# An attention and gated-MLP block on one core: the streamed gate and up weights are issued on GpSimd's queue, with other assumed landing times and another scheduling table

## The chip, the cores and the metric

The kernel runs on one NeuronCore of a Trainium2 chip. Its time is the device time of one execution in microseconds (us). A profile of one execution gives, for every engine, what ran when: PE is TensorE (matrix multiply), ACT is ScalarE (activation functions), DVE is VectorE (elementwise), POOL is GpSimd, SP is SyncE, which here issues nearly all DMAs.

## The reference

The block has 2048 tokens of width 512, 32 heads of 16, and a hidden width of 1792.

```python
mod = (silu(c) @ w_mod)            # six vectors of 512: sa, ca, ga, sb, cb, gb
h = layernorm(x) * (1 + ca) + sa
q, k, v = heads(h @ wqkv)          # 32 heads of 16
x = x + ga * (softmax(q k^T / 4) v) @ wo
h = layernorm(x) * (1 + cb) + sb
x = x + gb * ((gelu(h @ w_gate) * (h @ w_up)) @ w_down)
```

## The kernel before

**Scores and Exp.** For a set of 128 to 512 queries (`SETS`) and a group of four heads, PE makes scores, transposed, in tiles of 128 keys by 512 columns in PSUM (`ps_sc`, six banks). There are 2048 such tiles. Most go to ACT, which takes the Exp of two or three tiles in one instruction into `E` (`128x1024` or `128x1536`, line 377). The others go to DVE in groups of four ("quads"): DVE turns the four score tiles into 16-bit patterns that stand for powers of two (line 389, `128x512` from `ps_sc`, into `kq` buffers, which partly lie in the regions `dreg`, `mreg` and `onorm`), and three instructions of `128x2048` add a constant to those patterns (`sq` buffers). Each tile is then multiplied by the values on PE (`ps_pv`, from `E,vaug`, or from a DVE buffer and `vs`).

**Softmax sums.** A unit of four heads ends with a copy to `osb` and a chain: DMA of the sums to `den`, a reciprocal on DVE, a store to DRAM (`scr_rec`), four loads that spread it (`rb`), a product on DVE (`onorm`), and later four DMAs that merge head halves (`onorm<-onorm`). In semaphore names these are `db`, `dc`, `dd`, `de`.

**The MLP beside it.** When all of a query set's heads are done, its output projection, layer norm and MLP run on PE, ACT and DVE between the scores of later sets. For the first six sets (`FLOW`) gate and up weights are streamed: `load` in `side_ffn` fetches 256 columns (256 KB) into one of two buffers for each of the two matrices (`wst`, in `mreg`; semaphores `st...`), a new one each time PE has used a buffer up. Each of these sets fetches seven gate and seven up pieces. Later sets find their weights loaded.

**The order.** The program is written out in full by a planner. `stream` goes through the score tiles and keeps a model of when each engine is free and when each DMA has landed. It decides which tiles go to ACT and which to DVE, when a piece of MLP work is put between scores, and when a filler matmul (`xs,ident` or `xs,zero`, whose result is overwritten or nought) keeps PE going. `MARGIN` and `EARLY` add nanoseconds to the assumed landing time of a kind of DMA. `TUNE` holds one row of fourteen limits for each stage of 64 tiles. Engines carry out their rows strictly in order, and a row that waits for a semaphore holds up what stands behind it on its engine.

Of the kernel before, what the change touches and what calls it, by code (L numbers as in the profile page):

```python
# [13 lines left out]
P = 128  # L14
# [36 lines left out]
FLOW = sum(a + n <= 1536 for a, n in SETS)  # L51
ISSUE = {"dd": 462, "de": 630, "db": 610, "dc": 400, "st": 410, "sd": 530, "se": 530, "ws": 450, "wu": 420, "wg": 510, "wd": 480, "ou": 400, "qo": 620}
SAFE = 0
EARLY = (1500, 2500, 2000)
MARGIN = {"db": 1200, "dd": 1800, "de": 1500, "qo": 1500, "st": 1500, "sd": 1700, "se": 1700, "wd": 1700, "wu": 1500, "wg": 1500}
FIRST = (2, 1, 2, 3)
STOP = ('ln2',)
STOPAT = 0
# [2 lines left out]
STEP = 64  # L61
RULES = (600, 3500, 6, 120, 700, 150, 2, 9, 96, 30, 2, 1536, 100, 150)
TUNE = (
# [33 lines left out]
)  # L97
END = (0, None)
WAIT = 250
# [29 lines left out]
class _Recorder:  # L129
# [292 lines left out]
    def dma(self, eng, out, in_, sem, noncontig=False, late=0):  # L422
# [8 lines left out]
        run = min(int(a.ap[-1][1]) * mybir.dt.size(a.dtype) for a in (out, in_))  # L431
        return self.rec(eng, fn, [in_], [out], dma=sem, cost=(n, run, MARGIN.get(sem[:2], 0) + late))

# [36 lines left out]
class _Kernel(_Recorder):  # L470
# [696 lines left out]
    def side_ffn(self, gi, part=None):  # L1167
# [15 lines left out]
        def load(x, i):  # L1183
            if not flow or (i >= NFC // 2 and gi == FLOW - 1) or self.dry:
                return
            v = (self.B_w_gate, self.B_w_up)[x].rearrange("(a p) n -> p a n", p=P)
            b, k, i = (first + i) % 2, gi + i // (NFC // 2), i % (NFC // 2)
            self.task([("sp", lambda: self.dma("sp", self.wst[x][b], v[:, :, 2 * P * i:2 * P * i + 2 * P], "st%d%d" % (x, b)))],
                      ("wl", k, x, i))

        def load_down(i):
# [5 lines left out]
        if gi == 0:  # L1197
            yield from self.until(("wdg", 6))
            for i in range(2):
                load(0, i)  # L1200
                load(1, i)
# [4 lines left out]
        def up(x, ci, sub):  # L1206
            for s, fc in enumerate(sub):
                yield from self.until(("wl", gi, x, fc // 2) if flow else ("wr", x, fc // 2))
                for dci in range(NDC):
                    if flow:  # L1210
                        lhs = self.wst[x][(first + fc // 2) % 2][:, dci, P * (fc % 2):P * (fc % 2) + P]
                    else:
                        lhs = self.up_w((self.wg, self.wu)[x], fc, dci)
                    yield W, lambda s=s, lhs=lhs, dci=dci: self.mm(
                        mi[:, W * s:W * s + W], lhs, self.t2T[:, dci, c0:c0 + W], start=(dci == 0), stop=(dci == NDC - 1), whole=W == P)
                if fc % 2:
                    load(x, fc // 2 + 2)
# [220 lines left out]
    def rules(self, i):  # L1438
        self.tune = TUNE[min(i, len(TUNE) - 1)]

# [385 lines left out]
    def unit_end(self, u, acc):  # L1826
# [17 lines left out]
        sem = b + 4 * (o > 0)  # L1844
        late = EARLY if qd < 6 else (0, 0, 0)
        s2 = self.scr2[b, P * o:P * o + 4 * L]
# [261 lines left out]
```

## Time and profile before

| | |
|---|---|
| three executions | 808.4, 812.86, 815.13 us; median 812.86 |
| profiled execution | 810.3 us, of which 808.6 lie between its first and last instruction (the span) |
| granted TensorE clock | 0.996 |
| busy | PE 750.5 us (93%), DVE 752.3 (93%), ACT 776.8 (96%), POOL 4.6 (1%) |
| DMA | 60.92 MB, 75 GB/s on average |

The three shares are near each other. What sets the end is read from the chain of work that ended last and from the idle time of ACT in each stretch of the run.

### The profile page before, as it was taken

The numbers are of one execution on the slowest core, as the hardware profiler recorded it, in microseconds if no ns is written. First come the engines' busy times: TensorE is split into PE (matmuls) and PEld (weight loads), VectorE is DVE, ScalarE is ACT, GpSimd is POOL, SyncE is SP. The second block draws the span as 40 slices with busy tenths as digits, with TensorE's granted clock in tenths as the row PEclk, the third lists the DMA queues.
The fourth block names the chain that finished last, engine by engine and source line by source line (L and its number), as shares of the span: only waits on it lengthen the run. The fifth ranks groups of instructions, "written<-read, shape, count | busy, mean of one in ns | idle before, by whom it ended". The sixth has DMA issues, their size and how long they took to land.

```text
span 808.6 us, 37540 instructions
## 1 busy us (share of the span) xinstructions
PE 750.5 (93%) x17260; PEld 374.8 (46%) x17264; DVE 752.3 (93%) x1521; ACT 776.8 (96%) x734; POOL 4.6 (1%) x13
## 2 busy tenths in 40 slices
PE   8899999998989998999999999988999999989998
PEld 4333334433544454444543554344434554446666
DVE  7877899999999999999999999999998999999973
ACT  6999999999999999999999999999999999999972
POOL 2000000000000000000000000000000000000000
PEclk9999999999999999999999999999999999999999
DMA  9100112221541144104420442043223622200000
GB/s 295 66 15 8 25 50 74 75 58 32 148 145 29 39 128 134 34 16 133 129 65 16 140 121 54 22 128 114 62 64 104 189 83 76 71 10 13 18 12 15
DMA packets 97904, 60.92 MB, mean 75 GB/s; under 512 B 16913, under 2 KB 95378, under 8 KB 97746
## 3 DMA queue, kind: packets, MB, share of 16 engines
q1 hardware_dynamic: 97216, 57.99, 25.2%
q8 instruction: 135, 2.21, 1.1%
q10 hardware_dynamic: 530, 0.53, 0.2%
q14 instruction: 23, 0.19, 0.1%
HBM read 51.74 MB, written 4.18 MB: 69 GB/s over the span
## 4 chain that ended last, share of the span: by engine, by line
ACT 81%; PE 13%; DVE 3%; DMA 2%; issue 1%; SPq 0%; DVEq 0%
ACT E L377 78%; PE ps_sc L364 5%; PE ps_mi L364 4%; PE ps_pv L364 3%; ACT wreg L377 3%; DMA scr_rec<-rden 1%; DMA xs<-in_A_x_dram 0%; DVE mreg L389 0%; DMA mreg<-in_B_w_up_dram 0%; SPq L427 0%; DMA rb<-scr_rec 0%; DVE st L417 0%; DVE wreg L398 0%; DVE hreg L389 0%; PE ps_mi L368 0%
## 5 line engine op out<-in xcount | busy, mean ns | idle before, releaser
L377 ACT ACTIVATE E<-ps_sc 128x1024 bf16<-128x1024 f32 (+2 forms) x688 | 750.8, 1295 | 17.8 <-PE ps_sc L364 17.2
L364 PE MATMUL ps_sc<-qo,kT 32*128 32x256 bf16 (+2 forms) x2048 | 202.0, 273 | 19.8 <-ACT E L377 17.6
L364 PE MATMUL ps_sc<-qT,kT 32*128 32x256 bf16 (+3 forms) x2048 | 202.0, 274 | 17.7 <-ACT E L377 14.3
L364 PE MATMUL ps_pv<-E,vaug 128*17 128x256 bf16 (+2 forms) x3168 | 151.5, 274 | 2.7 <-DVE vaug L398 1.1
L389 DVE TENSOR_SCALAR dreg<-ps_sc 128x512 uint16<-128x512 f32 x204 | 138.2, 687 | 4.6 <-PE ps_sc L364 4.0
L364 PE MATMUL ps_mi<-wreg,mreg 128*32 128x256 bf16 x2816 | 110.0, 275 | 5.2 <-DVE wreg L398 1.7
L364 PEld LDWEIGHTS ps_sc<-qT,kT 32*128 32x128 bf16 (+1 forms) x2048 | 62.7, 92 | 109.8 <-ACT E L377 89.4
L364 PEld LDWEIGHTS ps_sc<-qo,kT 32*128 32x128 bf16 x2048 | 63.1, 92 | 106.5 <-ACT E L377 87.7
L364 PEld LDWEIGHTS ps_pv<-E,vaug 128*17 128x17 bf16 x3168 | 61.0, 89 | 58.9 <-issue 40.8
L389 DVE TENSOR_SCALAR kq<-ps_sc 128x512 uint16<-128x512 f32 x112 | 76.3, 688 | 8.0 <-PE ps_sc L364 7.4
L364 PEld LDWEIGHTS ps_mi<-wreg,mreg 128*32 128x32 bf16 x2816 | 64.1, 96 | 38.6 <-issue 21.5
L364 PE MATMUL ps_pv<-mreg,vs 128*17 128x256 bf16 (+2 forms) x1544 | 69.6, 267 | 0.5 <-issue 0.5
L389 DVE TENSOR_SCALAR mreg<-ps_sc 128x512 uint16<-128x512 f32 x100 | 67.7, 687 | 1.7 <-PE ps_sc L364 1.2
L389 DVE TENSOR_SCALAR mreg<-dreg 128x2048 uint16<-128x2048 uint16 x91 | 61.5, 686 | 0.0
L364 PEld LDWEIGHTS ps_pv<-mreg,vs 128*17 128x17 bf16 x1544 | 35.2, 91 | 9.6 <-issue 3.4
L364 PE MATMUL ps_mi<-hreg,wreg 128*32 128x512 bf16 (+1 forms) x496 | 37.3, 382 | 0.4 <-DVE vaug L398 0.2
L381 DVE TENSOR_TENSOR wreg<-wreg 128x1024 bf16<-128x1024 bf16 (+1 forms) x56 | 34.6, 618 | 0.0
L394 DVE SCALAR_TENSOR_TENSOR wreg<-wreg,ps_mi 128x512 bf16<-128x512 bf16 x49 | 33.5, 683 | 0.6 <-PE ps_mi L364 0.2
L398 DVE CAST wreg<-ps_mi 128x512 bf16<-128x512 f32 x49 | 33.6, 686 | 0.5 <-PE ps_mi L364 0.2
L389 DVE TENSOR_SCALAR mreg<-mreg 128x2048 uint16<-128x2048 uint16 x46 | 31.1, 684 | 0.0
L389 DVE TENSOR_SCALAR mreg<-kq 128x2048 uint16<-128x2048 uint16 x45 | 30.7, 686 | 0.1
L377 ACT ACTIVATE wreg<-wreg 128x1024 bf16<-128x1024 bf16 (+1 forms) x28 | 29.8, 1065 | 0.0
(202 smaller groups left out, 786.9 us busy)
## 6 DMA issues: line engine op xcount, KB each, us to landing
mreg<-in_B_w_up_dram SPq DMA_DIRECT2D x46, 256.0 KB, 3.1
mreg<-in_B_w_gate_dram SPq DMA_DIRECT2D x42, 256.0 KB, 3.7
dreg<-wd_scaled SPq DMA_DIRECT2D x18, 256.0 KB, 3.4
rb<-scr_rec SPq DMA_DIRECT2D x116, 32.0 KB, 2.0
mreg<-wd_scaled SPq DMA_DIRECT2D x12, 256.0 KB, 4.2
ereg<-wd_scaled SPq DMA_DIRECT2D x12, 256.0 KB, 4.1
mreg<-in_w_mod_dram SPq DMA_DIRECT2D x1, 2048.0 KB, 12.2
out_dram<-xs SPq DMA_DIRECT2D x15, 128.0 KB, 2.0
```

Source lines behind the costliest of these rows:

```text
L364: return self.rec("pe", lambda e: e.matmul(out, lhsT, rhs, start=start, stop=stop, tile_position=tp), [lhsT, rhs], [out], cost=(n, int(rhs ...
L377: return self.rec("act", lambda e: e.activation(out, in_, func, scale=scale, **kw), rd, wr, cost=self.cost("act", out, [in_], "act"))
L381: return self.rec(eng, lambda e: e.tensor_tensor(out, a, b, op), [a, b], [out], cost=self.cost(eng, out, [a, b], "tt"))
L389: return self.rec(eng, lambda e: e.tensor_scalar(out, a, s1, s2, **kw), rd, [out], cost=self.cost(eng, out, [a], "ts") + 60 * (len(rd) - 1 ...
L394: return self.rec("dve", lambda e: e.scalar_tensor_tensor(out, a, s, b, op0=op0, op1=op1), rd, [out], cost=self.cost("dve", out, [a, b], " ...
L398: return self.rec(eng, lambda e: e.tensor_copy(out, in_), [in_], [out], cost=self.cost(eng, out, [in_], "ts"))
```

## The change

Three things are edited. The DMA of a streamed gate or up piece is issued by GpSimd ("pool") instead of SyncE. The assumed landing times change: `EARLY`, which adds to the sums' DMAs of most units, falls; the store of the reciprocals (`dc`), the store of the scaled down weights (`ws`), the streamed pieces (`st`) and the streamed down weights (`sd`) get more. And the rows of `TUNE` are others (33 rows before and after; one line of each is shown).

```diff
-EARLY = (1500, 2500, 2000)
-MARGIN = {"db": 1200, "dd": 1800, "de": 1500, "qo": 1500, "st": 1500, "sd": 1700, "se": 1700, "wd": 1700, "wu": 1500, "wg": 1500}
+EARLY = (800, 1000, 800)
+MARGIN = {"db": 1200, "dd": 1800, "de": 1500, "qo": 1500, "st": 2300, "dc": 1500, "ws": 1500, "sd": 2000, "se": 1700, "wd": 1700, "wu": 1500, "wg": 1500}
...
 TUNE = (
+    (1000, 4097, 6, 120, 700, 150, 2, 9, 96, 30, 2, 1536, 100, 150),
...
-    (450, 4097, 6, 300, 1100, -100, 1, 9, 96, 30, 4, 1536, 100, 150),
...
-            self.task([("sp", lambda: self.dma("sp", self.wst[x][b], v[:, :, 2 * P * i:2 * P * i + 2 * P], "st%d%d" % (x, b)))],
+            self.task([("sp", lambda: self.dma("pool", self.wst[x][b], v[:, :, 2 * P * i:2 * P * i + 2 * P], "st%d%d" % (x, b)))],
```

Since the planner writes the whole program, nearly every stretch comes out in another order. Three places show what matters.

On SP, at the first query set's MLP, this is the difference between the two programs (`in_B_w_gate` and `in_B_w_up` are the streamed pieces, `wd_scaled` the down weights, `den` belongs to the chain of the sums, and `qo`, `qT` are copies that split the next queries into head halves):

```order
-L427 DMA mreg<-in_B_w_gate_dram 128x4x256
 L427 DMA dreg<-wd_scaled 128x2x512 x2
-L427 DMA mreg<-in_B_w_gate_dram 128x4x256
 L427 DMA onorm<-onorm 16x3x256 x4
-L427 DMA mreg<-in_B_w_gate_dram 128x4x256
 L427 DMA qo<-qT 16x4x256 x4
-L427 DMA mreg<-in_B_w_gate_dram 128x4x256
 L427 DMA dreg<-wd_scaled 128x2x512
 L427 DMA mreg<-wd_scaled 128x2x512
 L427 DMA den<-osb 128x1x16
 L427 DMA qT<-qo 16x4x256 x4
-L427 DMA mreg<-in_B_w_up_dram 128x4x256 x2
```

The streamed pieces no longer stand between the other DMAs of SP. On POOL, whose last work before was a small mask, the changed program goes on like this:

```order
L408 AFFINE_SELECT self<-self 128x128
L427 DMA mreg<-in_B_w_gate_dram 128x4x256
L427 DMA mreg<-in_B_w_up_dram 128x4x256
L427 DMA mreg<-in_B_w_gate_dram 128x4x256
L427 DMA mreg<-in_B_w_up_dram 128x4x256
L427 DMA mreg<-in_B_w_gate_dram 128x4x256 x4
L427 DMA mreg<-in_B_w_up_dram 128x4x256 x2
```

In all, 84 pieces (42 of gate, 42 of up) move from SP to POOL.

On ACT, these are the last Exp instructions ahead of the table load that precedes the end of the program, before:

```order
L377 ACTIVATE E<-ps_sc 128x1024 x4
L377 ACTIVATE E<-ps_sc 128x1536 x2
L377 ACTIVATE E<-ps_sc 128x1024 x4
L377 ACTIVATE E<-ps_sc 128x1536 x6
L377 ACT_TABLE_LOAD
```

and of the change:

```order
L377 ACTIVATE E<-ps_sc 128x1024 x7
L377 ACTIVATE E<-ps_sc 128x1536
L377 ACTIVATE E<-ps_sc 128x1024 x4
L377 ACTIVATE E<-ps_sc 128x1536 x8
L377 ACTIVATE E<-ps_sc 128x512
L377 ACT_TABLE_LOAD
```

More score tiles reach ACT here, and one Exp of a single tile is new. Over the whole program ACT has 389 Exp of 1024 columns (412 before), 287 of 1536 (268 before) and one of 512 that was not there; DVE has 408 conversions of a score tile (420 before) and 306 of its `128x2048` additions (315 before).

On PE, this stands between the last scores and the end of the last softmax products, before:

```order
L364 MATMUL ps_sc<-qo,kT 128x128 x12
L364 MATMUL ps_pv<-mreg,vs 17x128 x16
L368 MATMUL ps_mi<-ident,hreg 128x128 x2
L364 MATMUL ps_sc<-xs,ident 32x512 x4
L364 MATMUL ps_pv<-E,vaug 17x128 x32
L364 MATMUL ps_pv<-dreg,vaug 17x128 x16
L364 MATMUL ps_pv<-ereg,vs 17x128 x16
L364 MATMUL ps_pv<-mreg,vs 17x128 x16
L364 MATMUL ps_pv<-E,vaug 17x128 x16
L364 MATMUL ps_pv<-mreg,vs 17x128 x16
```

and of the change:

```order
L364 MATMUL ps_sc<-qo,kT 128x128 x4
L364 MATMUL ps_pv<-E,vaug 17x128 x16
L364 MATMUL ps_pv<-mreg,vs 17x128 x16
L368 MATMUL ps_mi<-ident,hreg 128x128 x2
L364 MATMUL ps_sc<-self,osb 128x4
L364 MATMUL ps_sc<-xs,ident 32x512 x4
L364 MATMUL ps_sc<-wo,onorm 32x512 x4
L364 MATMUL ps_pv<-E,vaug 17x128 x16
L364 MATMUL ps_pv<-ereg,vs 17x128 x16
```

Behind the last scores stand 64 products into `ps_pv` instead of 128.

58 rows, old and new, of the table TUNE are left out of this document.

## The prediction

> **What bounds the kernel now.** I read the profile's first part and its chain first, then each engine's busy time in ten stretches, then the rows that carry prices.
>
> ```profile
> PE 750.5 (93%) x17260; PEld 374.8 (46%) x17264; DVE 752.3 (93%) x1521; ACT 776.8 (96%) x734; POOL 4.6 (1%) x13
> ACT 81%; PE 13%; DVE 3%; DMA 2%; issue 1%; SPq 0%; DVEq 0%
> ```
>
> Three engines are nearly full, but the chain that ended last lies on ACT for 81% of the span. SP's queue has none of it to speak of. The stretches (columns: length, then busy us of PE, PEld, DVE, ACT, POOL) show where ACT is not busy:
>
> ```profile
> 0.00:13.26 13.26, 11.34 (x90) 5.57 (x95) 8.84 (x35) 6.15 (x14) 4.33 (x12) 1.00 0.91 259
> 13.26:100.00 86.74, 79.39 (x1412) 30.19 (x1407) 71.60 (x187) 85.64 (x79) 0.31 (x1) 0.98 0.17 53
> 100.00:200.00 100.00, 93.65 (x2149) 40.44 (x2145) 97.41 (x190) 100.00 (x93) 0.00 (x0) 1.00 0.22 61
> 200.00:300.00 100.00, 93.15 (x2242) 47.89 (x2246) 96.72 (x183) 98.80 (x94) 0.00 (x0) 1.00 0.34 97
> 300.00:400.00 100.00, 93.04 (x2213) 46.49 (x2201) 96.98 (x182) 99.81 (x94) 0.00 (x0) 1.00 0.32 91
> 400.00:500.00 100.00, 93.93 (x2180) 46.34 (x2180) 98.15 (x184) 100.00 (x96) 0.00 (x0) 1.00 0.29 79
> 500.00:600.00 100.00, 93.15 (x2160) 44.99 (x2156) 98.93 (x187) 100.00 (x96) 0.00 (x0) 1.00 0.28 76
> 600.00:700.00 100.00, 94.16 (x2130) 46.99 (x2126) 96.50 (x186) 98.68 (x92) 0.00 (x0) 0.98 0.35 101
> 700.00:781.25 81.25, 75.48 (x2382) 46.18 (x2375) 75.24 (x160) 80.58 (x73) 0.00 (x0) 1.00 0.10 26
> 781.25:808.60 27.35, 23.23 (x361) 19.76 (x351) 11.91 (x34) 7.10 (x13) 0.00 (x0) 1.00 0.04 12
> ```
>
> 13.26 is the start of the first Exp, 781.25 the table load behind the last one. Between them ACT is idle for 1.10 + 1.20 + 0.19 + 1.32 + 0.67 = 4.5 us out of 768. The head (13.3 us) and the end (27.4 us) are other chains. So **the span is head + ACT's work + 4.5 us + end**: a change gains at most 4.5 us by taking waits away, and anything above that must come out of ACT's work or the end.
>
> **The work that moves.** The new order has 412 - 23 Exp of 1024 columns, 268 + 19 of 1536 and one more of 512; that is 12 score tiles more on ACT and 12 fewer on DVE.
>
> ```profile
> L377 ACT ACTIVATE E<-ps_sc 128x1024 bf16<-128x1024 f32 x412 | 413.8, 1137 | 2.3 <-PE ps_sc L364 2.2
> L377 ACT ACTIVATE E<-ps_sc 128x1536 bf16<-128x1536 f32 x268 | 394.8, 1560 | 2.8 <-PE ps_sc L364 2.3
> L377 ACT ACTIVATE E<-ps_sc 128x512 bf16<-128x512 f32 x6 | 3.5, 598 | 9.4 <-PE ps_sc L364 9.4
> L377 ACT ACTIVATE E<-ps_sc 128x1024 bf16<-128x1024 f32 (+2 forms) x688 | 750.8, 1295 | 17.8 <-PE ps_sc L364 17.2
> ```
>
> Neighbours on ACT overlap: the two large forms' means add up to 412 x 1.137 + 268 x 1.560 = 886.5 us, while the group as a whole (last row, less 4 us for the small ones) is busy for 746.8. The overlap is 139.7 / 680 = 0.205 us each, so an instruction really costs 0.932 and 1.355 us, and a 512 one 0.598 - 0.205 = 0.393. The sum: -23 x 0.932 + 19 x 1.355 + 0.393 = **+4.7 us on ACT**. This is the bottleneck's own work and nothing hides it.
>
> ```profile
> L389 DVE TENSOR_SCALAR dreg<-ps_sc 128x512 uint16<-128x512 f32 x204 | 138.2, 687 | 4.6 <-PE ps_sc L364 4.0
> L389 DVE TENSOR_SCALAR mreg<-dreg 128x2048 uint16<-128x2048 uint16 x91 | 61.5, 686 | 0.0
> L364 PE MATMUL ps_sc<-xs,ident 128*32 128x512 bf16 x52 | 4.8, 386 | 1.6 <-ACT E L377 1.6
> ```
>
> DVE loses 12 conversions at 0.687 us and 9 additions at 0.686: **-14.4 us on DVE**, which gains nothing as long as ACT is fed. PE gets 48 more pieces of filler (36 in `ps_sc`, 12 in `ps_mi`), at 4.8 / 52 = 0.09 us each 4.4 us, in 58 us of PE's idle time. The planner puts fillers into score banks only where ACT's work reaches further than PE's, so more of them speak for a plan in which PE waits for ACT, not the reverse. At the end, 64 products into `ps_pv` fewer stand behind the last scores:
>
> ```profile
> 780.72 0.89 PE ps_pv L364 x63
> ```
>
> That row of the chain gives 0.89 / 63 = 0.014 us each: **-0.9 us**. The rest of the end has nearly the same rows.
>
> **The loads that move to POOL.** 84 issues leave SP.
>
> ```profile
> L427 SPq DMA_DIRECT2D mreg<-in_B_w_up_dram x46: 367/432/1385, 178.8 to 666.4; - x46
> DMA to landing us min/median/max: 2.8/3.1/5.5
> SPq L427 <- PE ps_mi L364: 62.3, 31, 7.2
> PE ps_mi L364 <- DMA mreg<-in_B_w_up_dram: 1.6, 1, 1.6
> PEld ps_mi L364 <- DMA mreg<-in_B_w_gate_dram: 0.6, 1, 0.6
> PE ps_mi L364 <- DMA mreg<-in_B_w_gate_dram: 0.3, 1, 0.3
> ```
>
> SP is spared about 84 x 0.432 = 36 us of issuing (duration: minimum, median, maximum ns) and most of 62.3 us in which such a load waited for PE to leave its buffer, with the sums' DMAs queued behind it. That is worth only what somebody waited for: PE waited for these weights three times, 2.5 us in all, though landings took up to 5.5 us. Behind a load on POOL stand only other such loads, and only PE waits for them. How long POOL takes to issue one, and how long it then takes to land, no row shows. Nearest are SP's 0.432 us and, for POOL's own work, 0.31 and 2.27 us:
>
> ```profile
> 55.77 0.31 POOL L408 TENSOR_SCALAR_AFFINE_SELECT self<-self 128x128 f32<-128x128 f32 x1 [50.48 <-DVE self L405]
> 2.17 2.27 POOL L405 MEMSET vaug<- 128x512 bf16 x1
> ```
>
> From below: the three waits go, at most 2.5 us gained. From above: each landing later by 2.27 - 0.43 = 1.8 us, which can cost PE 84 x 1.8 = 155 us if no load had slack. I take 0: two buffers per matrix give slack, as three waits in 84 loads show, and this price is nearest to SP's row, the same transfer. Both ends count for the range.
>
> **The other assumed landings.** `EARLY` and `MARGIN` move no data by themselves; they move rows. What was added over the sums' chain was 1200 + 1500 + 0 + 1800 + 2500 = 7.0 us, and is now 2.0 + 1.5 + 2.8 = 6.3.
>
> ```profile
> 221.47 4.71 DMA scr_rec<-rden
> 227.03 1.31 SPq L427
> 228.38 2.07 DMA rb<-scr_rec
> DVE onorm L381 <- DMA rb<-scr_rec: 1.2, 1, 1.2
> ```
>
> The first three rows, of the chain in order of time, show one late store and a busy SP queue behind it; DVE waited 1.2 us for it, the only such wait. If the plan now comes too early, DVE stands at `onorm`, with conversions queued behind it and ACT's score banks behind these: at worst 1.2 us for each of the 29 products, 35 us; at best the 1.2 us goes. I take 0, nearest to the one wait seen.
>
> **The sum.** 808.6 + 4.7 - 0.9 = 812.4 us of span, with today's 4.5 us of ACT's waits unchanged. The execution lasts 1.7 us longer than its span (810.3): 814.1 us. The profiled execution is 2.6 us below the median shown (812.86), so I put the forecast at 815.
>
> **A rule against the change.** A `128x2048` addition takes DVE 0.686 us, as long as 512 columns out of PSUM: a fourfold rate. The Trainium skill ("SBUF — State Buffer", Who interferes with whom) says that VectorE at such a rate and GpSimd lock one another out of a shared port pair for a whole instruction, and that descriptors which GpSimd writes for its own DMAs are starved by it. No run here has POOL and DVE so mixed; by it, loads land later or DVE stands, as the first rival has it.
>
> **Rivals.**
> 1. *DVE and POOL hold one another up* (slower). There are 105 x 3 = 315 additions between 100 and 781 us, 0.46 starts per us. If POOL kept DVE off for 0.43 us per load, the chance that at least one falls into it is 0.18 and its mean wait, half the time, 0.215: 84 x 0.18 x 0.215 = 3.3 us, below the 14.4 us that DVE is freed of. At 2.27 us it is 84 x 0.65 x 1.14 = 62 us. Half-way (1.35 us) 84 x 0.46 x 0.68 = 26 us, 12 more than DVE is freed of. DVE's idle time from 100 to 700 is only 15.3 us, so I let all 12 show, on top of 814: **826**. It decides from 14.4 / 84 = 0.17 us per load. For it: DVE is 97% busy there. Against: a third of DVE's time at most is such work.
> 2. *The plan no longer fits* (slower): loads or sums land later than the new order assumes. With a sixth of the loads waiting as long as the one at 1.6 us, 14 x 1.6 = 22 us of PE, of which ACT, one Exp ahead, sees the part beyond 1 us each, 8.4: **823**.
> 3. *SP's queue was what made ACT wait*: with it freed, all 4.5 us go: **810**. Against: DMA and SP are 2% of the chain.
> 4. *The move itself does nothing*, the weights being hidden either way: this is the forecast, where the table alone counts.
> 5. *Faster by over 1%*: 8.1 us below today needs 11.9 us less than the sum, and 4.5 is all that waits hold; the other 7.4 would have to come out of the end: **802**.
>
> **How the numbers follow.** Forecast 0.46 (own range 811 to 819), rival 3 0.12, rival 1 0.27, rival 2 0.10, rival 5 0.05. About 1% is what a measurement of this kernel can tell from no change. The forecast and rival 3 lie within it: same 0.58; rivals 1 and 2: slower 0.37; faster 0.05. The range goes from 809 (no waits left, 809.6) to 835, with rival 1's hold at about 1.8 us per load (84 x 0.56 x 0.9 = 42 us, 28 beyond what is freed, three quarters of it, 21, showing); what is beyond, with the faster case, is under 2 in 10.
>
> **What would show it.** ACT's busy time at 781 to 782, up 4.7; DVE's near 738 if POOL leaves it alone, and the mean of the `128x2048` additions still 0.686; ACT's idle time between first Exp and table load 3 to 8 us; POOL with 84 issues and landings near 3 to 4 us. I am wrong if additions or idle time on DVE grow, if PE waits for `in_B_w` DMAs more than 5 us in all, or if ACT's idle time passes 10 us.

## The result, and the profile after

The changed kernel takes 816.11 us (median of 19 executions, 813.79 to 818.87) against 811.45 us for the kernel before beside it (19 executions, 808.4 to 815.13): the ratio is 1.0057, with a 95% interval of 1.0044 to 1.0071. It is slower by 4.7 us, the difference of the medians, within the 1% that the prediction called the same. Times here are medians of the fast executions; one of the six of fewer_quads, further down, took 3435 us and is left out of its median.

These are the first part of the page of the changed kernel, its DMA queues, its chain, and the two large forms of Exp among the groups:

```profile
PE 751.3 (93%) x17211; PEld 374.4 (46%) x17211; DVE 742.8 (91%) x1500; ACT 781.7 (96%) x731; POOL 68.2 (8%) x97
q1 hardware_dynamic: 52864, 35.97, 15.9%
q0 software_dynamic: 6720, 22.03, 9.7%
ACT 81%; PE 13%; DVE 5%; issue 1%; DMA 0%; SPq 0%; DVEq 0%
L377 ACT ACTIVATE E<-ps_sc 128x1536 bf16<-128x1536 f32 x287 | 422.6, 1555 | 2.3 <-PE ps_sc L364 2.2
L377 ACT ACTIVATE E<-ps_sc 128x1024 bf16<-128x1024 f32 x389 | 393.9, 1138 | 2.7 <-PE ps_sc L364 2.2
```

ACT still holds 81% of the chain. Its busy time rose from 776.8 to 781.7 us, and DVE's fell from 752.3 to 742.8. POOL now shows 68.2 us, and 22 MB went through a queue of its own.

The stretch from the first Exp to the table load behind the last one, first of before, then of the changed kernel, and then the changed kernel's end (columns as in the prediction's stretches: length, busy us and count of PE, PEld, DVE, ACT, POOL, then granted clock, DMA share, GB/s):

```profile
13.26:781.25 767.99, 715.95 (x16829) 349.51 (x16827) 731.53 (x1452) 763.50 (x708) 0.31 (x1) 1.00 0.26 74
```

```profile
12.82:785.69 772.87, 718.28 (x16803) 350.03 (x16802) 721.89 (x1431) 768.43 (x705) 63.87 (x85) 1.00 0.27 74
785.69:812.10 26.41, 22.66 (x325) 19.05 (x317) 12.10 (x35) 7.13 (x13) 0.00 (x0) 1.00 0.04 12
```

ACT's idle time is length less busy: 767.99 - 763.50 = 4.49 us before and 772.87 - 768.43 = 4.44 after. So the span grew by ACT's own work, 768.43 - 763.50 = 4.93 us, less 0.94 at the end (27.35 to 26.41), 0.44 at the head (13.26 to 12.82) and 0.05 of idle time: 3.5 us, from 808.6 to 812.1. DVE's idle time in the same stretch grew from 767.99 - 731.53 = 36.5 us to 772.87 - 721.89 = 51.0.

The loads on POOL in the changed kernel (duration: minimum, median, maximum ns, first and last start), their landings, who waited for them, what POOL waited for most, and DVE's one wait for spread sums (1.2 us before):

```profile
L427 POOL DMA_DIRECT2D mreg<-in_B_w_gate_dram x42: 747/747/883, 175.7 to 645.4; - x42
L427 POOL DMA_DIRECT2D mreg<-in_B_w_up_dram x42: 747/747/1068, 176.6 to 660.8; - x42
DMA to landing us min/median/max: 3.2/3.5/5.5
PEld ps_mi L364 <- DMA mreg<-in_B_w_up_dram: 0.5, 1, 0.5
PE ps_mi L364 <- DMA mreg<-in_B_w_up_dram: 0.2, 1, 0.2
POOL mreg L427 <- PE ps_mi L364: 402.2, 73, 47.0
DVE onorm L381 <- DMA rb<-scr_rec: 0.4, 1, 0.4
```

An issue takes POOL 0.747 us, landings are much as they were on SP (before, 2.8 to 5.5 us for the up pieces and 2.7 to 6.1 for the tensor of the gate pieces), and PE hardly waits for streamed weights: the rows of 0.5 and 0.2 us are one load, waited for at 576.70 us by PE's weight loads and by PE. Of the three such rows of before, too, two are one load (at 373.27 us), so PE stood twice there, for 1.6 and at most 0.6 us, 2.2 and not 2.5 in all. POOL stands 402 us waiting for PE to leave buffers, which holds up nobody, since only such loads are behind them.

### The profile page after: what moved, and what is told of

Its sections match the earlier page's. It is cut to its first block, busy times and chain, and to the rows that moved or that the text cites. A ratio compares the mean times of both kernels' runs of the same rounds, so it can differ in the third digit from the quotient of the medians.

```text
span 812.1 us, 37411 instructions
## 1 busy us (share of the span) xinstructions
PE 751.3 (93%) x17211; PEld 374.4 (46%) x17211; DVE 742.8 (91%) x1500; ACT 781.7 (96%) x731; POOL 68.2 (8%) x97
## 3 DMA queue, kind: packets, MB, share of 16 engines
q1 hardware_dynamic: 52864, 35.97, 15.9%
q0 software_dynamic: 6720, 22.03, 9.7%
## 4 chain that ended last, share of the span: by engine, by line
ACT 81%; PE 13%; DVE 5%; issue 1%; DMA 0%; SPq 0%; DVEq 0%
ACT E L377 78%; PE ps_sc L364 5%; PE ps_mi L364 4%; PE ps_pv L364 3%; ACT wreg L377 2%; DVE mreg L389 1%; DVE dreg L389 1%; DVE wreg L398 1%; DVE wreg L381 0%; DMA xs<-in_A_x_dram 0%; DVE wreg L394 0%; DVE kq L389 0%; DVE st L417 0%; DVE xs L381 0%; DVE sq L389 0%
## 5 line engine op out<-in xcount | busy, mean ns | idle before, releaser
L377 ACT ACTIVATE E<-ps_sc 128x1024 bf16<-128x1024 f32 (+2 forms) x685 | 755.4, 1305 | 16.5 <-PE ps_sc L364 15.9
L364 PE MATMUL ps_sc<-qo,kT 32*128 32x256 bf16 (+2 forms) x2048 | 194.2, 273 | 21.0 <-ACT E L377 18.1
L364 PE MATMUL ps_sc<-qT,kT 32*128 32x256 bf16 (+3 forms) x2048 | 196.8, 273 | 16.2 <-ACT E L377 13.0
L364 PE MATMUL ps_pv<-E,vaug 128*17 128x256 bf16 (+2 forms) x3204 | 154.9, 272 | 1.6 <-DVE vaug L398 0.5
L389 DVE TENSOR_SCALAR dreg<-ps_sc 128x512 uint16<-128x512 f32 x200 | 134.9, 683 | 9.1 <-PE ps_sc L364 8.0
L389 DVE TENSOR_SCALAR kq<-ps_sc 128x512 uint16<-128x512 f32 x108 | 73.0, 683 | 9.7 <-PE ps_sc L364 8.9
L427 POOL DMA_DIRECT2D mreg<-in_B_w_gate_dram x42 | 31.6, 751 | 436.0 <-PE ps_mi L364 309.9
L364 PE MATMUL ps_pv<-mreg,vs 128*17 128x256 bf16 (+2 forms) x1472 | 65.1, 268 | 1.3 <-DVE mreg L389 1.0
L427 POOL DMA_DIRECT2D mreg<-in_B_w_up_dram x42 | 31.8, 757 | 104.9 <-PE ps_mi L364 92.3
L364 PEld LDWEIGHTS ps_pv<-mreg,vs 128*17 128x17 bf16 x1472 | 32.0, 91 | 13.2 <-DVE mreg L389 5.4
## 6 DMA issues: line engine op xcount, KB each, us to landing
mreg<-in_w_mod_dram SPq DMA_DIRECT2D x1, 2048.0 KB, 12.7
```

What stands on the lines that cost most here:

```text
L364: return self.rec("pe", lambda e: e.matmul(out, lhsT, rhs, start=start, stop=stop, tile_position=tp), [lhsT, rhs], [out], cost=(n, int(rhs ...
L377: return self.rec("act", lambda e: e.activation(out, in_, func, scale=scale, **kw), rd, wr, cost=self.cost("act", out, [in_], "act"))
L389: return self.rec(eng, lambda e: e.tensor_scalar(out, a, s1, s2, **kw), rd, [out], cost=self.cost(eng, out, [a], "ts") + 60 * (len(rd) - 1 ...
L427: return e.dma_start(out, in_)
```

## The experiments

The theory was that the queue move costs nothing, and that the time follows the plan: how many score tiles it gives ACT, and how long ACT waits in it. The rivals were that POOL's issues delay loads or DVE, and that freeing SP gives something back. In the kernels that keep an order, the planner counts the DMA on one queue while another issues it, so that PE, ACT and DVE get the same rows.

### The order of before, with POOL issuing (old_order_pool)

```diff
-self.dma("sp", self.wst[x][b], ...)
+self.dma("pool", self.wst[x][b], ..., plan="sp")
...
-        self.model(op, max(at, self.free[eng]), cost)
+        self.model(op, max(at, self.free[plan or eng]), cost, plan or eng)
```

> The order of before on PE, ACT, DVE and SP, with the 84 streamed pieces issued by POOL; the planner is told nothing of it. Theory A (ACT's work sets the time, the queue costs nothing): the time of before, ratio 0.998 to 1.002, ACT busy 776.8 us, additions of 128x2048 at 0.685 us but for a few that meet a POOL issue, 1 to 2 us in all. Theory B (POOL's issuing itself makes the 4.6 us, by blocked additions or late weights): ratio about 1.005.

It took 813.75 us (12 executions) against 811.09: 1.0028, interval 1.0012 to 1.0044. That lies between the two theories (at most 1.002, and 1.005). Its stretch from first Exp to table load, its waits for streamed weights, two links of its chain, and four microseconds around the second of them:

```profile
13.03:785.00 771.97, 718.10 (x16840) 349.81 (x16834) 732.02 (x1452) 763.89 (x709) 63.36 (x85) 0.99 0.27 74
PE ps_mi L364 <- DMA mreg<-in_B_w_up_dram: 1.8, 1, 1.8
PE ps_mi L364 <- DMA mreg<-in_B_w_gate_dram: 1.7, 1, 1.7
482.82 5.25 DMA mreg<-in_B_w_up_dram
630.21 7.14 DMA mreg<-in_B_w_gate_dram
630.00:632.00 2.00, 2.00 (x54) 1.24 (x52) 2.00 (x4) 2.00 (x3) 0.75 (x1) 1.00 1.03 339
632.00:634.00 2.00, 2.00 (x64) 1.13 (x56) 2.00 (x5) 2.00 (x3) 0.00 (x0) 1.00 1.10 352
```

ACT's work is that of before (763.89), and its idle time rose by 3.6 us to 771.97 - 763.89 = 8.08. Two loads, which hold 5.25 and 7.14 us of the chain, made PE wait 3.5 us, and ACT stood 3.2 us at these two places and right behind them; the median load lands within 3.5. The second load meets full DMA engines (a share of 1.03 and 1.10 at 339 and 352 GB/s): with the streamed pieces out of its queue, SP has issued seven transfers of the down weights from 626.2 to 630.1 us, ahead of it. In before the piece stood among them in SP's queue and landed in 4.1 us. So a queue of its own also takes away the order in which transfers start; no run tests this by itself, and why the first load is late stays open. In an order that allowed the loads 1500 ns above the modelled landing, the move costs about 2.3 us (0.0028 x 811); in the profiled execution, two late loads out of 84 account for most of the idle time that was added.

### The order of the change, with SP issuing (new_order_sp)

```diff
-self.dma("pool", self.wst[x][b], ...)
+self.dma("sp", self.wst[x][b], ..., plan="pool")
```

> The order of the changed kernel on PE, ACT and DVE, with the pieces back on SP at the place where the planner issued them. Theory A: the time of the change, ratio to before 1.004 to 1.007, ACT busy 781.7 us; if SP's queue gets jammed at places, up to 2 us more. Theory B: back to before, ratio 1.000.

It took 814.92 us (11 executions): 1.0043, interval 1.0025 to 1.0062, which overlaps that of the change. Its whole stretch, and then six microseconds of it and the same six of the changed kernel:

```profile
12.99:787.91 774.92, 719.58 (x16803) 350.85 (x16802) 721.55 (x1431) 769.12 (x705) 0.56 (x1) 1.00 0.26 74
610.00:612.00 2.00, 1.28 (x27) 0.47 (x28) 1.86 (x5) 2.00 (x3) 0.00 (x0) 0.94 0.69 224
612.00:614.00 2.00, 2.00 (x26) 0.53 (x18) 1.43 (x4) 1.38 (x3) 0.00 (x0) 0.50 0.00 0
614.00:616.00 2.00, 2.00 (x32) 0.57 (x31) 1.83 (x3) 1.84 (x2) 0.00 (x0) 0.71 0.00 0
```

```profile
610.00:612.00 2.00, 1.48 (x35) 0.58 (x32) 2.00 (x4) 2.00 (x3) 0.00 (x0) 1.00 0.15 48
612.00:614.00 2.00, 1.87 (x35) 0.65 (x36) 2.00 (x4) 2.00 (x4) 0.00 (x0) 1.00 0.00 0
614.00:616.00 2.00, 1.72 (x40) 0.65 (x36) 2.00 (x6) 2.00 (x3) 0.00 (x0) 1.00 0.00 0
```

ACT is idle for 774.92 - 769.12 = 5.80 us here, 1.36 more than in the changed kernel, and no load is late. The difference lies in places like the one shown: PE's clock falls to half for some 3.4 us, PE then fills the whole stretch with the same work, and ACT loses 0.62 + 0.16 us. Such a fall stands at 89 us too; in one-microsecond stretches ACT is idle for 1.32 us in both together. The profiled execution of the change has none. Without them the two idle times agree (5.80 - 1.32 = 4.48 and 4.44), so in this order the queue makes no difference that these runs can tell.

### Four issues for each load (pool_four_issues)

```diff
+            if parts > 1:
+                return [e.dma_start(out[:, y, :], in_[:, y, :]) for y in range(parts)]
             return e.dma_start(out, in_)
...
-self.dma("pool", self.wst[x][b], ...)
+self.dma("pool", self.wst[x][b], ..., parts=4)
```

This is the changed kernel with 336 issues of 64 KB instead of 84 of 256 KB, in the same order.

> The order of the changed kernel, with each streamed piece issued by POOL in four DMAs of 64 KB (336 issues, about 252 us of POOL). Theory A: each issue has a window of about 0.2 us in which an addition on DVE must wait; 6 of 84 met it in the change, so some 24 of 336 here, 5 us of DVE's time, which DVE's idle time takes; pieces land about 2.2 us later, which the two buffers mostly cover. Ratio to before 1.005 to 1.010. The rule of the port lock for a whole instruction: an addition that falls into an issue waits for up to 0.75 us, 336 x 0.29 x 0.37 = 36 us more on DVE, ratio 1.02 or more.

It took 815.77 us (7 executions): 1.0054, interval 1.0032 to 1.0076. Its stretch, and one of its issues with the addition beside it:

```profile
12.97:788.28 775.31, 719.94 (x16803) 351.09 (x16802) 722.48 (x1431) 768.80 (x705) 195.50 (x337) 1.00 0.27 74
385.92 1.03 POOL L428 DMA_DIRECT2D mreg<-in_B_w_up_dram  x1
386.14 0.69 DVE L389 TENSOR_SCALAR hreg<-dreg 128x2048 uint16<-128x2048 uint16 x1
```

POOL's time tripled (195.50 us against 63.87), and DVE's rose by 0.6 us (722.48 against 721.89). One addition of `128x2048` took over 0.8 us and seven took over 0.73, where some 24 had been expected; the changed kernel has six over 0.8. PE waited for three streamed loads, 2.1 us in all, instead of one. The expectation of additions held up was wrong, and rival 1 of the prediction with it: more of POOL's issuing does not cost DVE in proportion.

The hold goes mostly the other way. An issue of 64 KB takes 0.537 us at the median, but 67 of the 336 took longer and ended 0.12 us (0.118 to 0.129) after the end of an addition, as in the rows (385.92 + 1.03 = 386.95, against 386.14 + 0.69 = 386.83). They cost POOL 16 us in all. So POOL's issue stands until DVE's whole addition is over, while an addition stood at most 0.13 us for an issue of 64 KB.

### Everything but the queue, and the same order with POOL issuing (all_but_queue, best_order_pool)

The first is the change with the loads left on SP, planned anew. The second has the first one's rows on PE, ACT and DVE, with the loads on POOL.

```diff
-self.dma("pool", self.wst[x][b], ...)
+self.dma("sp", self.wst[x][b], ...)
...
+self.dma("pool", self.wst[x][b], ..., plan="sp")
```

> New table and new assumed landing times, pieces on SP as before, planned anew. It puts 4 score tiles more on ACT than before (393, 282 and 1 more Exp; 1.2 us of work by the prices of the prediction) and has no more filler than before. Theory A: ratio 1.000 to 1.003, so that of the change's 4.7 us most come from planning this table with POOL's queue. A theory that the table or the landing times are bad in themselves: ratio 1.005 or more.

> The order on PE, ACT and DVE is that of the run in which everything but the queue is taken from the change (all_but_queue); here GpSimd issues the streamed gate and up pieces, and the planner goes on counting those DMAs on SyncE's queue. It leaves out nothing. Theory A, the plan and not the move makes the time: ACT's work stays at 764.3 us within 1, its idle time between 2 and 4 us, and the ratio is between 0.995 and 0.997. Rival B, the move costs by itself what it cost in the order of before (late loads, +2.3 us): ACT's work the same, its idle time 4 to 6 us, PE waits 2 to 4 us for in_B_w_gate and in_B_w_up, and the ratio is about 0.998. Rival C, the move costs what all_but_queue and the changed kernel differ by (8.4 us): ratio about 1.006.

They took 807.68 us (9 executions; 0.9954, interval 0.9935 to 0.9973) and 807.74 us (12 executions; 0.9957, 0.9933 to 0.9982). Both are about 0.45% below before, and no theory had all_but_queue that fast (1.000 at the least). Its expectation also counts an Exp of 512 columns too many: the trace has six, as before. Their stretches from first Exp to table load, in this order:

```profile
12.75:779.01 766.26, 716.13 (x16815) 349.68 (x16808) 728.68 (x1449) 764.26 (x704) 0.56 (x1) 1.00 0.26 75
```

```profile
13.10:779.01 765.91, 715.78 (x16815) 349.70 (x16811) 729.30 (x1449) 764.27 (x703) 64.08 (x85) 1.00 0.26 75
12.00:300.00 288.00, 268.10 (x5801) 118.31 (x5799) 269.05 (x564) 286.61 (x265) 19.07 (x25) 1.00 0.25 72
700.00:780.00 80.00, 75.71 (x2385) 47.60 (x2380) 72.83 (x158) 79.70 (x71) 0.00 (x0) 1.00 0.06 13
```

And the same last two stretches of the changed kernel:

```profile
12.00:300.00 288.00, 268.09 (x5808) 118.48 (x5810) 269.10 (x564) 286.75 (x266) 18.94 (x25) 1.00 0.25 72
700.00:780.00 80.00, 72.62 (x2225) 43.81 (x2227) 69.28 (x142) 77.58 (x70) 0.00 (x0) 1.00 0.06 13
```

The two queues give the same work (764.26 and 764.27 us on ACT), idle times of 2.00 and 1.64 us, and the same time. The move itself costs nothing here that these runs can tell. The span of all_but_queue, 804.4 us, is 4.2 below that of before: 0.8 more of ACT's work, 2.5 less of its idle time, 1.9 less at the end and 0.5 at the head. The changed kernel has the same table, landing times and queue as best_order_pool. Only what the planner was told of the queue differs, and it is 8.4 us slower (816.11 - 807.74): in the profiles 768.43 - 764.27 = 4.2 us more work on ACT, 4.44 - 1.64 = 2.8 more idle time, and about one at the end, less 0.3 at the head. On ACT the two programs have the same first 380 instructions, up to 411 us (the stretch to 300 us shows it: 286.75 and 286.61 us busy), and there they part. The plan of the change then gives ACT eight tiles more (389 x 2 + 287 x 3 + 1 = 1640, against 393 x 2 + 282 x 3 = 1632), and has 2.42 us of ACT's idle time between 700 and 780 us, against 0.30, where no streamed load is left.

### Fewer tiles on DVE (fewer_quads)

```diff
-                            and keyed(cand[0])
+                            and keyed(cand[0]) and quads_begun < 1 + 99 * pos / nseq
...
-                        rnd = rounds[cand.pop(0)]
+                        rnd = rounds[cand.pop(0)]; quads_begun += 1
```

This is the kernel before with a limit on how many groups of four DVE may have begun by each place, so that ACT gets 24 tiles more (374 Exp of 1024, 301 of 1536, one more of 512).

> Before, with one edit: a group of four score tiles may go to DVE only as long as fewer than 1 + 99 x (share of the tiles done) have gone. DVE gets 99 groups and not 105, ACT 24 tiles more: 374, 301 and 1 more Exp, by the prices of the prediction 9.7 us of work. Theory A (ACT's work sets the time): 8 to 12 us longer, ratio 1.010 to 1.015, ACT's idle time between the first Exp and the table load staying at 3 to 7 us. Rival (PE and DVE set the time as much as ACT does, so that what leaves DVE comes back): ratio 1.000 to 1.005.

It took 817.97 us (5 executions) against 810.7: 1.0097, interval 1.0074 to 1.0119. That is 7.3 us, just under the 8 to 12 expected, and well above the rival's 1.005. Its stretch:

```profile
13.02:791.95 778.93, 717.83 (x16751) 349.09 (x16749) 712.30 (x1411) 773.42 (x705) 0.31 (x1) 1.00 0.26 73
```

By the prediction's prices 38 Exp of 1024 fewer, 33 of 1536 more and one of 512 are -38 x 0.932 + 33 x 1.355 + 0.393 = 9.7 us; ACT's work rose by 773.42 - 763.50 = 9.9, and the span by 9.4. Time does follow ACT's tiles: 0.41 us of work each in the profile, and 7.3 / 24 = 0.30 us by the medians.

### One part of the change alone, each planned anew

queue_only has only the edit of the queue, margins_only only those of `EARLY` and `MARGIN`, and table_only only that of `TUNE`.

> Before, with the streamed pieces issued by POOL and the planner told so, its table and assumed landing times unchanged. 8 tiles more on ACT (389, 286, none more): 2.9 us of work. Theory A: ratio 1.003 to 1.008, the upper end if ACT's idle time rises as it did in the old order with POOL (8.1 us). If freeing SP's queue is worth something by itself: 1.000 or less.

> Before, with the new EARLY and MARGIN alone. 16 tiles more on ACT (376, 297 and 1 more Exp): 6.1 us of work. Theory A: ratio 1.006 to 1.010. If the assumed landing times were what made the all-but-queue kernel faster than before: 0.995 to 1.000.

> Before, with the new table alone. 8 tiles more on ACT (393, 283 and 1 more Exp): 3.0 us of work. Theory A: ratio 1.003 to 1.007. If the table by itself made the all-but-queue kernel faster than before: 0.995 to 1.000.

Their stretches, in this order:

```profile
12.72:794.01 781.29, 722.41 (x16875) 351.03 (x16869) 727.03 (x1436) 768.30 (x703) 63.60 (x85) 0.99 0.26 73
```

```profile
13.07:793.03 779.96, 721.67 (x16780) 351.74 (x16776) 718.72 (x1425) 771.32 (x703) 0.31 (x1) 1.00 0.26 74
```

```profile
13.36:789.68 776.32, 720.43 (x16815) 349.78 (x16810) 724.50 (x1436) 767.72 (x705) 0.56 (x1) 1.00 0.26 73
```

| | time, us | ratio and interval | ACT's work above before | ACT idle |
|---|---|---|---|---|
| queue_only | 820.24 | 1.0114, 1.0089 to 1.0139 | 4.8 | 13.0 |
| margins_only | 822.22 | 1.0135, 1.0113 to 1.0157 | 7.8 | 8.6 |
| table_only | 817.04 | 1.0075, 1.0056 to 1.0094 | 4.2 | 8.6 |
| the change | 816.11 | 1.0057, 1.0044 to 1.0071 | 4.9 | 4.4 |

All three came out slower than expected (table_only by little), because ACT's idle time was put too low, and because its work too came out 1.2 to 1.9 us above the prices (2.9, 6.1 and 3.0). A price net of overlap holds only while neighbours overlap, and in queue_only ACT goes idle 31 times against 15 in before; this reason is argued, not tested. Each part alone is slower than all three together. That a row of limits that fits one set of assumed landings makes another choice under another is argued; no run looks at a single row. In queue_only there is a second cause, seen in its timeline and in stretches of two microseconds:

```profile
534.63 0.75 POOL L427 DMA_DIRECT2D mreg<-in_B_w_gate_dram  x1 [45.01 <-PE ps_mi L364]
541.02 0.83 PE L364 MATMUL ps_mi<-wreg,mreg 128*32 128x256 bf16 x12 [1.66 <-DMA mreg<-in_B_w_gate_dram]
542.44 1.45 ACT L377 ACTIVATE E<-ps_sc 128x1536 bf16<-128x1536 f32 x1 [2.23 <-PE ps_sc L364]
```

```profile
540.00:542.00 2.00, 0.98 (x18) 0.43 (x18) 0.58 (x1) 0.21 (x1) 0.00 (x0) 0.68 0.21 74
542.00:544.00 2.00, 2.00 (x32) 0.74 (x26) 0.37 (x1) 1.45 (x1) 0.11 (x1) 0.50 0.05 12
544.00:546.00 2.00, 2.00 (x37) 0.91 (x38) 1.97 (x4) 1.83 (x2) 0.65 (x1) 0.50 0.28 59
```

The load issued at 534.63 us lands 6.3 us later, PE stands for 1.66 us and ACT behind it for 2.23 (until 542.44, in the second stretch); the clock falls to half over the same microseconds, and ACT loses 0.28 us more while PE catches up. Here too the DMA engines are full while the load is under way, a share of 1.01 from 536 to 540 us, and SP issues four transfers of the down weights from 534.28 to 535.77.

## Why the prediction was right

**ACT's work is the span's main term: right.** 4.7 us were predicted from twelve tiles and their net prices, and 4.93 measured; fewer_quads gives 9.9 for 9.7 at twice the number of tiles. The other plans bound how good the price is: 0.8 for 1.2 in all_but_queue, and 4.8 for 2.9 in queue_only. The same order also comes out at 768.43 to 769.12 us in three kernels, so an agreement within 0.2 us is partly luck.

**The end: right**, -0.94 us for the predicted -0.9. The head's -0.44 was not foreseen; over all these kernels the first Exp starts between 12.7 and 13.4 us, so it is scatter.

**"Today's 4.5 us of ACT's waits unchanged": right in size only.** The prediction had no term for falls of PE's clock. This is where they stand in the profile of before:

```profile
88.00:90.00 2.00, 1.88 (x22) 0.62 (x22) 1.96 (x6) 2.00 (x3) 0.00 (x0) 0.72 0.00 0
90.00:92.00 2.00, 2.00 (x18) 0.30 (x19) 1.31 (x4) 2.00 (x2) 0.00 (x0) 0.50 0.00 0
92.00:94.00 2.00, 2.00 (x33) 0.66 (x35) 1.45 (x5) 1.57 (x3) 0.00 (x0) 0.93 0.04 8
...
620.00:622.00 2.00, 1.41 (x17) 0.71 (x19) 1.64 (x5) 2.00 (x3) 0.00 (x0) 0.84 0.05 4
622.00:624.00 2.00, 2.00 (x32) 0.64 (x36) 1.33 (x3) 1.59 (x2) 0.00 (x0) 0.50 0.30 57
624.00:626.00 2.00, 2.00 (x52) 1.14 (x51) 1.23 (x2) 1.59 (x2) 0.00 (x0) 0.81 0.48 145
```

Two falls hold 0.43 + 0.41 + 0.41 = 1.25 of the 4.49 us. In the profiled execution of the change there are none, and 4.44 us are all waits of the plan. Each execution records its mean clock, so a straight line of time against clock can be put through each kernel's executions and read at full clock (its standard error there is 0.9 us for old_order_pool, 0.6 for new_order_sp and 0.2 to 0.3 for the others):

| | executions | mean clock | median, us | at full clock, us |
|---|---|---|---|---|
| before | 54 | 0.9955 | 810.9 | 808.3 |
| the change | 19 | 0.9986 | 816.1 | 815.1 |
| old_order_pool | 12 | 0.9958 | 813.8 | 811.1 |
| new_order_sp | 11 | 0.9983 | 814.9 | 813.9 |
| all_but_queue | 9 | 0.9986 | 807.7 | 806.9 |
| best_order_pool | 12 | 0.9988 | 807.7 | 807.3 |

The line of before is 6.8 us for 0.01 of clock. At full clock the change is 6.8 us behind (815.1 - 808.3), not the 3.8 of the sum; a clock that falls less often, 0.0031 x 680 = 2.1 us, gives part of it back. The line says that the two go together, not that the clock is the cause: one fall lowers the mean clock by 3.4 x 0.5 / 808.6 = 0.0021, for which the line has 1.4 us, while the two falls of before hold 0.6 us of ACT's idle time each. The forecast of 815 against 816.1 thus rests on a sum without the clock on either side. It also rests on a choice that was given no reason: the profiled execution lay 2.6 us below the median shown, and the forecast took up 0.9 of them. Beside the 19 executions the median of before is 811.45, 1.15 above the profiled one; that the choice fits is luck. The profiled execution of the change is also the shortest of its 19, so its fit with the predicted span (812.1 for 812.4) flatters the sum. Of the 2.3 us up to the median, 1.0 goes with the clock by this line; the rest stays open.

**A sign that was named came true, and did not mean what it was to mean.** The prediction called itself wrong if idle time on DVE grew, and it grew by 14.5 us. But DVE lost 9.6 us of work in a stretch that is 4.9 us longer, and ACT was fed as before (4.44 us idle). Idle time on an engine that was relieved of work shows nothing by itself; the additions, the other half of that sign, kept their mean (0.683 us, 0.685 before).

**The move taken at nothing: right for this order, not in general.** At full clock the queue is worth 815.1 - 813.9 = 1.2 us, 807.3 - 806.9 = 0.4 and 811.1 - 808.3 = 2.8 in the three orders; only the last is told apart from nothing, by its ratio. Two buffers for each matrix were slack enough in the change, and PE's waits fell from two to one, of 0.5 us at most (the prediction's "three times, 2.5 us" counts one load twice); in the old order two loads were late, one of them behind transfers that SP could now issue ahead of it. That was the price bounded as "each landing later", and it is 1.0 to 3.6 us by the ratio's interval, not 155.

**Rival 4, "the table alone counts": wrong in its words.** table_only gave 817.04, near the change, but with 8.6 us of idle time. The queue counts too, less through the chip than through the plan: what the planner is told of it is worth 8.4 us. **Rival 2, "the plan no longer fits",** did not come true for the change. Of the three parts alone it fits queue_only, where PE waits 2.9 us for streamed pieces and DVE 1.1 for sums. In margins_only only DVE waits for such a DMA, 0.4 us, and in table_only nobody does, so that their 8.6 us of idle time lie in the order itself, with ACT waiting for PE's scores and no late landing; the prediction had no rival for that. **Rival 3** is out: falls of the clock aside, freeing SP made ACT's idle time in the same order smaller by 0.4 us at most (1.64 against 2.00).

**Rival 1, and the rule of the Trainium skill ("SBUF — State Buffer", Who interferes with whom).** The timeline of the changed kernel shows the two engines meet:

```profile
221.28 0.75 POOL L427 DMA_DIRECT2D mreg<-in_B_w_gate_dram  x1 [1.91 <-PE ps_mi L364]
221.62 0.89 DVE L389 TENSOR_SCALAR sq<-mreg 128x2048 uint16<-128x2048 uint16 x1
```

An addition that starts 0.34 us after POOL's issue takes 0.89 us instead of 0.683. Of 306 additions 27 lay beside an issue, and six were held up: all that began between 0.3 and 0.5 us after the issue (five at 0.345 to 0.349 us, one at 0.428, which took 0.81). They cost DVE 1.2 us in all, 1.2 / 84 = 0.014 us for a load, where 0.17 would have decided. In the other direction an addition that began 0.09 us after an issue went with the longest one, 1.068 us. So the two do lock one another out. The rule speaks of a whole instruction; that holds where DVE holds POOL, as the issues of pool_four_issues show, which end 0.12 us after the addition, but DVE was kept off for 0.2 us of POOL's 0.747 only. The starving of descriptors that it names shows just as such a delay of single issues: here 80 of 84 took 0.747 to 0.749 us.

**DVE -14.4: wrong, it was -9.6** in the main stretch (731.53 to 721.89) for 21 instructions. The step that failed took 0.686 us for each, as an instruction lasts alone, though ACT's prices had been taken net of overlap. DVE's neighbours overlap too: in the timeline of before, seven instructions in a row, most of them such, start 0.60 us apart from 57.02 to 60.62 us. That makes 21 x 0.60 = 12.6 us; the net saving was 9.64 / 21 = 0.46 us each, and (731.53 - 712.30) / 42 = 0.46 in fewer_quads, which has 24 conversions and 18 additions fewer. Of the 3 us between 12.6 and 9.64, held additions are 1.2, and the rest stays open. DVE was not the bound, so it cost the forecast nothing, but rival 1's reserve of 14.4 us was half too large.

## What to carry to other kernels

In a program that a planner writes out, first count what the plan gives the bounding engine, at net prices (a group's busy time, not its mean), and only then ask what the moved instruction costs. A planner's assumptions and its table of limits belong together: to try an edit of the hardware's side, hold the order fixed and change only who issues. Moving a transfer to another queue also lets those behind it start earlier, so look at what then shares the DMA engines with the one that was moved. And compare granted clocks over several executions before reading anything into one or two microseconds of a single profile.

## What had not been expected of the hardware

PE's clock falls to half in pieces of about 3.4 us (summed over stretches of one microsecond, old_order_pool's three falls give 10.2 us at half rate, before's two 6.8). In the trace's record of the clock the two falls of before start 156.0 such lengths of 3.413 us apart, and those of new_order_sp 153.0. PE need not stand still for it: in new_order_sp PE was busy for 1.28 of the 2 us in which the clock first fell, and in the changed kernel the same place, with 1.48 of 2 us, passed at full clock. The Trainium skill ("TensorE: Matmul & The Clock Gate", What's actually happening) has the same length, a free-running window of about 3.4 us; what share of work within it decides, no run here shows.

On POOL's queue a load of 256 KB goes in larger packets: 6720 packets for 22.03 MB are 3.3 KB each, whereas the packets of SP's queue fell by 97216 - 52864 = 44352 for the same bytes, about 500 B each:

```profile
q1 hardware_dynamic: 97216, 57.99, 25.2%
```

That is the row of before. The share of DMA time stayed the same, 25.2% then and 15.9 + 9.7 = 25.6% now, so the fewer packets gained nothing. Splitting a load in four cost POOL 0.537 us for an issue of 64 KB against 0.747 for 256 KB:

```profile
L428 POOL DMA_DIRECT2D mreg<-in_B_w_gate_dram x168: 537/537/1018, 175.8 to 652.1; - x168
```

Most of an issue's time is thus independent of its size: by these two points about 0.47 us of it, an estimate.
